# Attention product in 64x64 tiles, FFN products regrouped around x's transposes, and a new order of block 0

## The chip, the cores and the metric

One program runs on one core of a Trainium2 chip. The metric is the device time of one execution in microseconds. The core's engines have instruction queues of their own and wait for each other by semaphores: TensorE (PE, matmuls and transposes; PEld is its loading of weights), VectorE (DVE), ScalarE (ACT), GpSimd (POOL), and SyncE (SP), which here issues the loads and stores.

## What is computed

An attention without softmax, then an FFN with a gate, all in float32:

```python
# q, k, v: (8, 8, 576, 64); x: (4608, 512); d_ff 1536
kv = einsum('bhsd,bhse->bhde', k, v)          # 64x64 for each batch and head
out = einsum('bhsd,bhde->bhse', q, kv)
rms = sqrt(mean(out * out, axis=-1) + 1e-6)
attn = out / rms * g_norm
x = attn.transpose(0, 2, 1, 3).reshape(4608, 512)
g = x @ w_gate
y = (g * sigmoid(g) * (x @ w_val)) @ w_out
```

The three weights come as float64 and are rounded to float32 on the chip.

## The kernel before

The 4608 tokens go through in nine blocks of 512 (`BLK`), four row tiles of 128 each. Since a batch has 576 tokens, block n is cut: in the odd blocks, one row tile of 128 tokens belongs to two batches, 64 tokens each (`parts`).

**Attention of a block** (class `Att`): `load` brings k, v and q; `kv` forms the 64x64 products of k and v, two heads side by side; `turn_q` transposes q; `product(i)` forms q times kv for half a block (i is 0 or 1, two row tiles), squares it on ACT, sums the squares on DVE (`z`) and calls `root`, a chain of eleven short DVE operations that gives 1/sqrt in `y`; then DVE scales the product, out of PSUM, into `xt`. `turn_x(i)` transposes `xt` on PE, and ACT writes it to `x`, which the FFN reads. `sums` forms four sums and differences of quarters of x on DVE.

**FFN of blocks 1 to 8**: seven products of quarter matrices replace eight (Strassen's scheme in Winograd's form). `Up` has a group of seven for each 256 columns of d_ff, `Down` one group for the block, with 12 matmuls of 256 columns in each product. `Down` runs its products in the order 1, 5, 6, 2, 7, 4, 3, and after each one `down` takes one step of the next block's attention from a list (`late`). Differences of weights (tile `t`) are subtracted on GpSimd into six buffers, each as soon as PE has read the older one.

**FFN of block 0** is plain (`plain_up`, `plain_down`), because its weights are still being rounded meanwhile. A piece of weights is 128 columns (or rows of w_out); `Words.round_to` needs two ACT and four DVE operations for it. `t2` then forms one weight sum in place, which the scheme of the later blocks needs.

**What sets the order.** Instructions are emitted in the order of the code, and the framework's scheduler then orders each engine's queue by its own estimates; the engines run their queues strictly in that order. Tiles come from pools: `ld` has seven buffers for every load; PSUM has eight banks, one in pool a, two each in b and c, three in m. All loads are issued on SP in one queue.

Of the kernel before, what the change touches and what calls it, by code (L numbers as in the profile page):

```python
# [18 lines left out]
def kernel(  # L19
# [156 lines left out]
    def round_w(name, j):  # L176
        dst = wviews[name][0]
        words.pop((name, j)).round_to(dst[:, j : j + 1, :] if name == "o" else dst[:, :, P * j : P * (j + 1)])

    class Att:  # L180


        def __init__(self, n):
            self.n = n

            self.cut, half = divmod(n, 2)
            self.split = half * D

        def parts(self, t):
# [7 lines left out]

        def load(self):
            n = self.n
            self.k, self.v, self.q = [], [], []  # L200
            if n < B:
                for j in range(NS):
                    hs = slice(2 * j, 2 * j + 2)
                    for tiles, src in ((self.k, k), (self.v, v)):
                        t = ld_pool.tile([P, 2 * BLK], F32, name="ld")
                        t = t[0:KP, 0 : 2 * KT * D].rearrange("p (h x) -> p h x", h=2)
                        nc.sync.dma_start(
                            out=t, in_=src[n, hs].rearrange("h (p t) d -> p h (t d)", t=KT)
                        )
                        tiles.append(t.rearrange("p h (t d) -> p h t d", t=KT))  # L210
# [36 lines left out]

        def product(self, i):

            ps = [m_psum.tile([P, 2, NS, D], F32, name="m") for _ in range(2)]
            for t in range(2):
                for j in range(NS):
                    for b, _, p0, p1 in self.parts(2 * i + t):
                        for u in range(2):
                            rows = slice(u * D, (u + 1) * D)
                            nc.tensor.matmul(  # L259
                                ps[u][p0:p1, t, j, :], lhsT=self.qt[rows, 2 * i + t, j, p0:p1],  # L260
                                rhs=kvs[b % 3][rows, j, :], start=True, stop=True,
                            )
            z = st_pool.tile([P, 2, 2, NS], F32, name="z")
            for u in range(2):
                sq = sq_pool.tile([P, 2, NS, D], F32, name="sq")
                nc.scalar.activation(out=sq, in_=ps[u], func=ACT.Square)  # L266
                nc.vector.tensor_reduce(out=z[:, u], in_=sq, axis=mybir.AxisListType.X, op=OP.add)  # L267
            y = self.root(z)
            xt = xt_pool.tile([P, 2, NS, 2, D], F32, name="xt")
            for u in range(2):  # L270
                mul(nc.vector, xt[:, :, :, u], ps[u], y[:, u].unsqueeze(3).to_broadcast([P, 2, NS, D]))
            self.xt = xt

        def root(self, z):

            nc.vector.tensor_scalar(out=z, in0=z, scalar1=1.0 / D, scalar2=eps, op0=OP.mult, op1=OP.add)
            y = st_pool.tile([P, 2, 2, NS], F32, name="y")
            nc.vector.tensor_scalar(  # L278
                out=y.bitcast(I32), in0=z.bitcast(I32), scalar1=-0.5, scalar2=float(0x5F3759DF),
                op0=OP.mult, op1=OP.add,  # L280
            )
            a = st_pool.tile([P, 2, 2, NS], F32, name="a")
            for _ in range(3):
                nc.vector.scalar_tensor_tensor(out=a, in0=y, scalar=-0.5, in1=y, op0=OP.mult, op1=OP.mult)  # L284
                nc.vector.tensor_tensor(out=a, in0=a, in1=z, op=OP.mult)  # L285
                nc.vector.scalar_tensor_tensor(out=y, in0=a, scalar=1.5, in1=y, op0=OP.add, op1=OP.mult)  # L286
            return y

# [14 lines left out]
        def sums(self):  # L303
# [52 lines left out]
    class Up(Quad):  # L356
        def __init__(self, ffn, j):
            super().__init__(2)
            self.ffn, self.j = ffn, j
            x, att = ffn.att.x, ffn.att  # L360
            fs = slice(2 * P * j, 2 * P * (j + 1))
            b11, b21, t2, b22 = wg[:, 0:2, fs], wg[:, 2:4, fs], wv[:, 0:2, fs], wv[:, 2:4, fs]
            a11, a12, s2, a22 = x[:, 0:2, 0:HB], x[:, 2:4, 0:HB], x[:, 0:2, HB:BLK], x[:, 2:4, HB:BLK]
# [91 lines left out]
    class Ffn:  # L455
# [28 lines left out]
        def down(self, fill):  # L484
            down = self.down_
            for p in (1, 5, 6, 2, 7, 4, 3):
# [4 lines left out]
                down.multiply(p)  # L491
                if fill:
                    fill.pop(0)()

        def plain_up(self, f):
            ps = []
            for pool, w in ((b_psum, wg), (c_psum, wv)):
                ps.append(pool.tile([P, BLK], F32, name=pool.name[0]))  # L500
                for i in range(NS):
                    nc.tensor.matmul(
                        ps[-1], lhsT=w[:, i, P * f : P * (f + 1)], rhs=self.att.x[:, i, :],
                        start=(i == 0), stop=(i == NS - 1),
                    )
# [35 lines left out]
    blocks = [Att(n) for n in range(NB)]  # L541
    blocks[0].load()
    weights(4)
    for steps in blocks[0].steps():
        for step in steps:
            step()

    for n in range(NB):
        ffn = Ffn(n, blocks[n])
        kv, turn, late = blocks[n + 1].steps() if n + 1 < NB else ([], [], [])  # L550
        if n == 0:
            for f in range(NF):
                weights(2 * (f + 2))
                ffn.plain_up(f)
            weights(len(pieces))
            blocks[1].load()
            for step in kv + turn:
                step()
            for j in range(NP):
                fs = slice(2 * P * j, 2 * P * (j + 1))  # L560
# [45 lines left out]
```

## Time and profile before

| | |
|---|---|
| time, median of 3 runs | 1191.09 us (1190.01 to 1192.87) |
| the profiled execution | 1190.74 us; its span 1189.0 us |
| mean granted clock of TensorE | 0.976 |
| PE busy | 1122.0 us, 94% of the span |
| DVE busy | 404.4 us, 34% |
| ACT busy | 274.5 us, 23% |
| GpSimd busy | 401.7 us, 34% |
| HBM read | 47.19 MB |

In the views quoted below, a timeline row has its start and its duration in us, engine, line, operation, output and inputs, then what ended the engine's idle time before it, in brackets. Equal instructions that follow each other are one row (x24). A float32 matmul leaves two records. A row of windows has the stretch, PE's busy time in it, the granted clock of TensorE, the DMA engines' busy share and GB/s.

### The profile page before, as it was taken

Reading aid. Unit: us, or ns where it says so; the run is one execution under the profiler, and the core shown is the slowest. Engines: PE = TensorE matmul, PEld = TensorE weight load, DVE = VectorE, ACT = ScalarE, POOL = GpSimd, SP = SyncE. Lnnn points to the kernel's source line nnn. Section 1 sums busy time; section 2 is a strip of 40 time slices with the busy share of each in tenths; the row PEclk is TensorE's granted clock in tenths of the full one; section 3 lists DMA queues with packets and bytes.
Section 4 is the critical chain, followed back from the end, with each engine's and each line's share of the span. In section 5 each row is a group of like instructions: output and inputs, shape, how many; then the busy total and the mean of one; then the engine's idle time right before and its main releaser. Section 6 shows DMA issues by size and latency. Waiting matters only on the chain.

```text
span 1189.0 us, 14539 instructions
## 1 busy us (share of the span) xinstructions
PE 1122.0 (94%) x6016; PEld 919.8 (77%) x6016; DVE 404.4 (34%) x770; ACT 274.5 (23%) x468; POOL 401.7 (34%) x320
## 2 busy tenths in 40 slices
PE   3699999998999899998999899989998999999998
PEld 3344456887888788887888788878887888788887
DVE  3466962223321431234112512233214312431221
ACT  3244521221122212221222112211221122112210
POOL 0000221542245324442445145422443245423550
PEclk8699999999999999999999999999999999999999
DMA  9344650210003000400031002100030000000000
GB/s 269 94 141 142 181 128 18 56 41 21 36 19 77 20 19 18 96 21 1 36 86 31 1 36 56 41 20 36 13 69 1 19 18 1 1 1 36 1 1 35
DMA packets 70241, 57.55 MB, mean 48 GB/s; under 512 B 39456, under 2 KB 64032, under 8 KB 70176
## 3 DMA queue, kind: packets, MB, share of 16 engines
q1 hardware_dynamic: 70112, 56.63, 17.6%
q8 instruction: 47, 0.77, 0.3%
q14 instruction: 18, 0.15, 0.0%
q0 software_dynamic: 64, 0.00, 0.0%
HBM read 47.19 MB, written 9.44 MB: 48 GB/s over the span
## 4 chain that ended last, share of the span: by engine, by line
PE 79%; DVE 7%; issue 1%; ACT 1%; DMA 0%; DVEq 0%
PE b L339 43%; PE c L339 18%; PE a L339 8%; PE b L515 3%; PE m L259 3%; DVE y L286 2%; PE m L297 2%; PE m L228 2%; DVE z L267 1%; PE m L242 1%; DVE xt L112 1%; DVE y L278 1%; ACT sq L266 1%; DVE a L284 1%; DVE a L285 1%
## 5 line engine op out<-in xcount | busy, mean ns | idle before, releaser
L111 POOL TENSOR_TENSOR t<-wv 128x512 f32<-128x512 f32 x48 | 66.3, 1382 | 395.9 <-PE b L339 170.7
L111 POOL TENSOR_TENSOR t<-wg,wv 128x512 f32<-128x512 f32 x96 | 123.0, 1285 | 178.1 <-PE c L339 90.6
L111 POOL TENSOR_TENSOR t<-wo 128x512 f32<-128x512 f32 x72 | 91.2, 1267 | 127.5 <-PE c L339 76.3
L110 DVE TENSOR_TENSOR s<-h 128x256 f32<-128x256 f32 x48 | 20.4, 425 | 307.8 <-POOL h L112 307.8
L339 PE MATMUL b<-wo,h 128*128 128x256 f32 x384 | 94.6, 406 | 0.0
L339 PE MATMUL b<-x,wg 128*128 128x256 f32 x384 | 93.1, 382 | 0.0
L339 PE MATMUL b<-x,t 128*128 128x256 f32 x384 | 91.3, 381 | 0.8
L339 PE MATMUL b<-x,wv 128*128 128x256 f32 x384 | 90.7, 379 | 0.0
L339 PE MATMUL c<-xs,t 128*128 128x256 f32 x384 | 90.7, 379 | 0.0
L339 PE MATMUL c<-xs,wv 128*128 128x256 f32 x384 | 90.7, 379 | 0.0
L339 PE MATMUL b<-xs,t 128*128 128x256 f32 x384 | 90.7, 379 | 0.0
L339 PE MATMUL a<-x,wg 128*128 128x256 f32 x384 | 90.7, 379 | 0.0
L339 PEld LDWEIGHTS b<-wo,h 128*128 128x128 f32 x384 | 78.5, 208 | 12.0 <-POOL h L112 0.3
L110 DVE TENSOR_TENSOR u<-c,u 128x512 f32<-128x512 f32 x96 | 65.9, 687 | 63.2 <-ACT u L382 63.2
L339 PE MATMUL b<-t,h 128*128 128x256 f32 x384 | 86.3, 381 | 0.8 <-ACT u L444 0.8
L339 PEld LDWEIGHTS b<-x,t 128*128 128x128 f32 x384 | 72.3, 190 | 12.0 <-issue 2.5
L339 PEld LDWEIGHTS b<-t,h 128*128 128x128 f32 x384 | 71.8, 190 | 12.7 <-issue 3.6
L339 PEld LDWEIGHTS c<-xs,t 128*128 128x128 f32 x384 | 73.0, 190 | 9.9
L339 PEld LDWEIGHTS b<-x,wv 128*128 128x128 f32 x384 | 73.0, 190 | 9.9
L339 PEld LDWEIGHTS a<-x,wg 128*128 128x128 f32 x384 | 73.0, 190 | 9.9
L339 PEld LDWEIGHTS b<-xs,t 128*128 128x128 f32 x384 | 73.0, 190 | 9.9
L339 PEld LDWEIGHTS c<-xs,wv 128*128 128x128 f32 x384 | 73.0, 190 | 9.9
(74 smaller groups left out, 1450.4 us busy)
## 6 DMA issues: line engine op xcount, KB each, us to landing
ld<-in_k_dram SPq DMA_DIRECT2D x32, 288.0 KB, 4.4
ld<-in_v_dram SPq DMA_DIRECT2D x32, 288.0 KB, 3.4
out_dram<-o SPq DMA_DIRECT2D x18, 512.0 KB, 2.8
ld<-in_q_dram SPq DMA_DIRECT2D x32, 256.0 KB, 4.9
ld<-in_moe_w_gate_dram SPq DMA_DIRECT2D x12, 512.0 KB, 6.2
ld<-in_moe_w_val_dram SPq DMA_DIRECT2D x12, 512.0 KB, 4.8
ld<-in_moe_w_out_dram SPq DMA_DIRECT2D x12, 512.0 KB, 3.6
ld<-in_q_dram SPq DMA_DIRECT2D x8, 128.0 KB, 4.2
```

The source lines that it names most:

```text
L110: add = lambda e, o, a, b: e.tensor_tensor(out=o, in0=a, in1=b, op=OP.add)
L111: sub = lambda e, o, a, b: e.tensor_tensor(out=o, in0=a, in1=b, op=OP.subtract)
L112: mul = lambda e, o, a, b: e.tensor_tensor(out=o, in0=a, in1=b, op=OP.mult)
L228: nc.tensor.matmul(self.kv_ps[u * D : (u + 1) * D, j, :], lhsT=self.k[j][:, u, c, :], rhs=self.v[j][:, u, c, :], start=(c == 0), stop=(c = ...
L242: nc.tensor.transpose(ps[:, j], self.q[t][:, j], ident)
L259: nc.tensor.matmul(ps[u][p0:p1, t, j, :], lhsT=self.qt[rows, 2 * i + t, j, p0:p1], rhs=kvs[b % 3][rows, j, :], start=True, stop=True,)
L266: nc.scalar.activation(out=sq, in_=ps[u], func=ACT.Square)
L267: nc.vector.tensor_reduce(out=z[:, u], in_=sq, axis=mybir.AxisListType.X, op=OP.add)
L286: nc.vector.scalar_tensor_tensor(out=y, in0=a, scalar=1.5, in1=y, op0=OP.add, op1=OP.mult)
L297: nc.tensor.transpose(ps[:, e, t], xt[:, t, j + e], ident)
L339: nc.tensor.matmul(self.ps[name][:, e], lhsT=lhsT, rhs=rhs, start=first and (e, i) == (0, 0), stop=i == self.steps - 1, skip_group_check=True,
L515: nc.tensor.matmul(ps, lhsT=self.h[:, f, P * t : P * (t + 1)], rhs=wo[:, f, :], start=(f == 0), stop=(f == NF - 1),)
```

## The change

1. **Product**: every piece of the attention product is cut into output tiles of 64 rows, so that a matmul has 64x64 weights. 16 matmuls of a row tile stand where there were 8.
2. **The list of steps in `Down`**: `half(0)` (product, root, scaling), nothing, `turn_x(0)`, `half(1)`, nothing, and then `turn_x(1)` with `sums`. By the code, two products of the FFN stand between a half and its transposes; before, it was one.
3. **Block 0's attention**: q is loaded ahead of k and v (in every block). In block 0, k and v go to the room of `h` and need no `ld` buffer. `all` runs both halves of the attention at once: one root over both, the second product in banks of pools b and c. One piece of weights is rounded ahead of it, where there were four; the others are to follow the last scaling (`issue_after`).
4. **Weights in tiles**: `wg` and `wv` are six tiles of 256 columns each, no longer one.
5. **Down part of block 0**: `t2` and the first `plain_down` stand ahead of block 1's `kv` and `turn_q`.

PE's queue in the down part of block 1 (`b`, `c`, `a`: PSUM of the FFN's products, in the order 1, 5, 6, 2, 7, 4, 3; `m`: PSUM of the attention; a row counts matmuls). Before:

```order
L339 MATMUL b<-wo,h 128x256 x12
L259 MATMUL m<-kv_112,qt 128x64 x8
L259 MATMUL m<-kv_113,qt 128x64 x8
L339 MATMUL c<-t,s_1189 128x256 x12
L297 MATMUL m<-ident,xt 128x128 x8
L339 MATMUL b<-wo,h 128x256 x12
L259 MATMUL m<-kv_113,qt 128x64 x16
L339 MATMUL a<-wo,h 128x256 x12
L297 MATMUL m<-ident,xt 128x128 x8
L339 MATMUL b<-t,h 128x256 x12
L339 MATMUL b<-x,wg 128x256 x2
L339 MATMUL b<-t,h 128x256 x12
```

The same place now:

```order
L378 MATMUL b<-wo,h 128x256 x12
L271 MATMUL m<-kv_112,qt 64x64 x16
L271 MATMUL m<-kv_113,qt 64x64 x16
L378 MATMUL c<-t,s_1234 128x256 x12
L378 MATMUL b<-wo,h 128x256 x12
L315 MATMUL m<-ident,xt 128x128 x8
L378 MATMUL a<-wo,h 128x256 x12
L271 MATMUL m<-kv_113,qt 64x64 x32
L378 MATMUL b<-t,h 128x256 x12
L378 MATMUL b<-x,wg_114 128x256
L315 MATMUL m<-ident,xt 128x128 x3
L378 MATMUL b<-t,h 128x256 x12
```

The first half's transposes moved behind product 6; of the second half's, three stand behind product 7 and one matmul of the next block, ahead of product 4, and the other five (not shown) behind product 4. It is so in all of blocks 1 to 7.

DVE's queue at the second half of the same block. Before, at that half's end (`y`: the root's last step; `xt`: scaling; `o`, `h`: work behind product 2; `xs`: sums of x):

```order
L286 SCALAR_TENSOR_TENSOR y<-a,y 128x16
L112 TENSOR_TENSOR xt<-m,y 128x8x64 x2
L110 TENSOR_TENSOR o_1543<-a,s 128x2x256
L111 TENSOR_TENSOR h<-h 128x6x256
L110 TENSOR_TENSOR xs<-x 128x512
```

And now, from the first half's scaling to the second half's start (`z`: sums of squares):

```order
L111 TENSOR_TENSOR xt<-m,y 128x8x64 x2
L109 TENSOR_TENSOR o_1588<-a,s 128x2x256
L110 TENSOR_TENSOR h<-h 128x6x256
L281 TENSOR_REDUCE z<-sq 128x8 x2
L287 TENSOR_SCALAR z<-z 128x16
L290 TENSOR_SCALAR y<-z 128x16
```

Product 2's addition into `o` and subtraction on `h` stood behind the second half's scaling; now they stand ahead of its reductions.

DVE's queue in block 0's attention (`a`, `y`: root; `u`, `g`: steps of rounding). Before, in the middle of the first half's root:

```order
L284 SCALAR_TENSOR_TENSOR a<-y 128x16
L150 TENSOR_SCALAR g<-ld 128x512
L285 TENSOR_TENSOR a<-a,z 128x16
L151 SCALAR_TENSOR_TENSOR u_391<-u_391,g 128x512
L286 SCALAR_TENSOR_TENSOR y<-a,y 128x16
L145 TENSOR_SCALAR u_402<-u_402 128x512
L284 SCALAR_TENSOR_TENSOR a<-y 128x16
L150 TENSOR_SCALAR g<-ld 128x512
```

Now, from the last steps of the one root on:

```order
L297 SCALAR_TENSOR_TENSOR a<-y 128x32
L298 TENSOR_TENSOR a<-a,z 128x32
L299 SCALAR_TENSOR_TENSOR y<-a,y 128x32
L111 TENSOR_TENSOR xt<-m,y 128x8x64 x2
L111 TENSOR_TENSOR xt<-b,y 128x8x64
L111 TENSOR_TENSOR xt<-c,y 128x8x64
L144 TENSOR_SCALAR u_366<-u_366 128x512
L149 TENSOR_SCALAR g<-ld 128x512
```

No rounding stands among the root's steps any more; it follows the four scalings, but for the first piece's four operations, which stand ahead of the reductions.

The diff, cut:

```diff
-    wg = consts.tile([P, NS, FF], F32, name="wg")
-    wv = consts.tile([P, NS, FF], F32, name="wv")
+    wg, wv = ([consts.tile([P, NS, 2 * P], F32, name=f"{x}{j}") for j in range(NP)] for x in ("wg", "wv"))
...
+        def load(self, room=None):
+            self.load_q()
...
+                for i, (tiles, src) in enumerate(((self.k, k), (self.v, v))):
+                    if room:
+                        t = room.rearrange("p f t -> p (f t)")[:, (2 * j + i) * 2 * KT * D :]
+                    else:
                         t = ld_pool.tile([P, 2 * BLK], F32, name="ld")
...
-        def product(self, i):
-            ps = [m_psum.tile([P, 2, NS, D], F32, name="m") for _ in range(2)]
+        def product(self, i, pools=None):
+            pools = pools or (m_psum, m_psum)
+            self.ps[i] = [pool.tile([P, 2, NS, D], F32, name=pool.name[0]) for pool in pools]
...
                     for b, _, p0, p1 in self.parts(2 * i + t):
-                        for u in range(2):
-                            rows = slice(u * D, (u + 1) * D)
-                            nc.tensor.matmul(
-                                ps[u][p0:p1, t, j, :], lhsT=self.qt[rows, 2 * i + t, j, p0:p1],
-                                rhs=kvs[b % 3][rows, j, :], start=True, stop=True,
-                            )
+                        for p in range(p0, p1, D):
+                            for u in range(2):
+                                rows = slice(u * D, (u + 1) * D)
+                                nc.tensor.matmul(
+                                    self.ps[i][u][p : p + D, t, j, :],
+                                    lhsT=self.qt[rows, 2 * i + t, j, p : p + D], rhs=kvs[b % 3][rows, j, :],
+                                    start=True, stop=True,
+                                )
...
+        def half(self, i):
+            self.product(i)
+            self.root(i)
+            self.scale(i)
+
+        def all(self):
+            for i in range(2):
+                self.turn_q(i)
+            self.kv(range(NS))
+            self.product(0)
+            self.product(1, (b_psum, c_psum))
+            self.root(0, 2)
+            for i in range(2):
+                self.scale(i)
+                self.turn_x(i)
+            return self.scaled
...
-            late = [
-                lambda: self.product(0), lambda: self.turn_x(0), lambda: self.product(1), lambda: self.turn_x(1),
-            ]
-            return kv, turn, late + ([self.sums] if self.n else [])
+            def last():
+                self.turn_x(1)
+                if self.n:
+                    self.sums()
+            return kv, turn, [lambda: self.half(0), None, lambda: self.turn_x(0), lambda: self.half(1), None, last]
...
-    blocks[0].load()
-    weights(4)
-    for steps in blocks[0].steps():
-        for step in steps:
-            step()
+    room = h_pool.tile([P, NF, BLK], F32, name="h")
+    blocks[0].load(room)
+    weights(1)
+    scaled = blocks[0].all()
...
-                weights(2 * (f + 2))
+                with tc.issue_after(scaled.ins):
+                    weights(2 * (f + 2))
                 ffn.plain_up(f)
             weights(len(pieces))
             blocks[1].load()
+            for j in range(NP):
+                t2(wv[j][:, 0:2], wv[j][:, 2:4], wg[j][:, 0:2])
+            ffn.plain_down(0)
             for step in kv + turn:
                 step()
-            for j in range(NP):
-                fs = slice(2 * P * j, 2 * P * (j + 1))
-                t2(wv[:, 0:2, fs], wv[:, 2:4, fs], wg[:, 0:2, fs])
-            for t in range(T):
+            for t in range(1, T):
                 ffn.plain_down(t)
-                for step in late[2 * t : 2 * t + 2]:
-                    step()
+                for step in late[2 * t - 2 : 2 * t]:
+                    if step:
+                        step()
```

More of the change, by code (lines that the diff above doesn't have):

```diff
@@ L187, in __init__ @@
             self.split = half * D
+            self.ps, self.z = {}, None
         def parts(self, t):
@@ L196, in parts, with load_q @@
             return [(n, first, 0, P)]
[L198 to L204, printed above, removed]
-                        t = ld_pool.tile([P, 2 * BLK], F32, name="ld")
-                        t = t[0:KP, 0 : 2 * KT * D].rearrange("p (h x) -> p h x", h=2)
-                        nc.sync.dma_start(
-                            out=t, in_=src[n, hs].rearrange("h (p t) d -> p h (t d)", t=KT)
-                        )
-                        tiles.append(t.rearrange("p h (t d) -> p h t d", t=KT))
+        def load(self, room=None):
+            self.load_q()
+            self.k, self.v = [], []
+            if self.n == B:
+                return
+            for j in range(NS):
+                hs = slice(2 * j, 2 * j + 2)
+                for i, (tiles, src) in enumerate(((self.k, k), (self.v, v))):
+                    if room:
+                        t = room.rearrange("p f t -> p (f t)")[:, (2 * j + i) * 2 * KT * D :]
+                    else:
+                        t = ld_pool.tile([P, 2 * BLK], F32, name="ld")
+                    t = t[0:KP, 0 : 2 * KT * D].rearrange("p (h x) -> p h x", h=2)
+                    nc.sync.dma_start(out=t, in_=src[self.n, hs].rearrange("h (p t) d -> p h (t d)", t=KT))
+                    tiles.append(t.rearrange("p h (t d) -> p h t d", t=KT))
+        def load_q(self):
+            self.q = []
             for i in range(2):
@@ L281, in root @@
             )
-            a = st_pool.tile([P, 2, 2, NS], F32, name="a")
+            flat = lambda t: t.rearrange("p i u t j -> p (i u t j)")
+            y, a, z = flat(y), flat(a), flat(z)
             for _ in range(3):
@@ L286, in root, with scale @@
                 nc.vector.scalar_tensor_tensor(out=y, in0=a, scalar=1.5, in1=y, op0=OP.add, op1=OP.mult)
-            return y
+        def scale(self, i):
+            self.xt = xt_pool.tile([P, 2, NS, 2, D], F32, name="xt")
+            for u in range(2):
+                y = self.y[:, i, u].unsqueeze(3).to_broadcast([P, 2, NS, D])
+                self.scaled = mul(nc.vector, self.xt[:, :, :, u], self.ps[i][u], y)
         def turn_x(self, i):
@@ L491, in down @@
                 down.multiply(p)
-                if fill:
-                    fill.pop(0)()
+                step = fill.pop(0) if fill else None
+                if step:
+                    step()
         def plain_up(self, f):
```

32 lines of the change are left out of this document (16 added, 16 removed).

## The prediction

> **What bounds the kernel now.** I read the page first, its busy times and the chain that ended last:
> ```profile
> PE 1122.0 (94%) x6016; PEld 919.8 (77%) x6016; DVE 404.4 (34%) x770; ACT 274.5 (23%) x468; POOL 401.7 (34%) x320
> ...
> PE 79%; DVE 7%; issue 1%; ACT 1%; DMA 0%; DVEq 0%
> ```
> PE bounds the kernel, so time comes off only where it idles, runs slowly or has less to do. The list of its waits (us in total, times, longest) says where it idles:
> ```profile
> PE m L297 <- DVE xt L112: 47.5, 15, 14.6
> PE m L228 <- DMA ld<-in_v_dram: 12.7, 6, 5.4
> ```
> Nearly all idle time stands before x's transposes (L297), which wait for VectorE's scaled `xt`. The rest waits for v. The timeline of the lead-in and of block 0:
> ```profile
> 13.36 1.55 PE L228 MATMUL m<-ld 96*64 96x64 f32 x24 [0.92 <-DMA ld<-in_v_dram]
> ...
> 35.20 1.94 PE L297 MATMUL m<-ident,xt 128*128 128x128 f32 x8 [14.62 <-DVE xt L112]
> ...
> 37.07 3.68 PE L259 MATMUL m<-kv,qt 64*128 64x64 f32 x32
> ...
> 46.53 1.94 PE L297 MATMUL m<-ident,xt 128*128 128x128 f32 x8 [5.78 <-DVE xt L112]
> ...
> 48.39 5.66 PE L502 MATMUL b<-x,wg 128*128 128x512 f32 x8
> ...
> 53.89 3.60 PE L502 MATMUL c<-x,wv 128*128 128x512 f32 x8
> ...
> 134.12 1.88 PE L515 MATMUL b<-wo,h 128*128 128x512 f32 x4
> 138.38 0.92 PE L228 MATMUL m<-ld 96*64 96x64 f32 x24 [2.38 <-DMA ld<-in_v_dram]
> ...
> 150.10 0.92 PE L228 MATMUL m<-ld 96*64 96x64 f32 x24 [1.64 <-DMA ld<-in_v_dram]
> ...
> 192.85 1.89 PE L339 MATMUL b<-x,wg 128*128 128x256 f32 x8
> ```
> The FFN starts only at 48.4, its down part at 134.1, block 1's at 192.9. In each of blocks 1 to 7 the down part then looks like this (block 1):
> ```profile
> 278.17 5.45 PE L339 MATMUL c<-t,s 128*128 128x256 f32 x24
> ...
> 280.31 1.26 POOL L111 TENSOR_TENSOR t<-wo 128x512 f32<-128x512 f32 x1 [6.95 <-PE c L339]
> 280.42 1.18 DVE L278 TENSOR_SCALAR y<-z 128x16 int32<-128x16 int32 x1
> ...
> 282.04 1.26 POOL L111 TENSOR_TENSOR t<-wo 128x512 f32<-128x512 f32 x1 [0.46 <-PE c L339]
> 282.06 1.27 DVE L286 SCALAR_TENSOR_TENSOR y<-a,y 128x16 f32<-128x16 f32 x1
> ...
> 285.79 1.29 DVE L112 TENSOR_TENSOR xt<-m,y 128x512 f32<-128x512 f32 x2
> ...
> 287.23 1.32 PE L297 MATMUL m<-ident,xt 128*128 128x128 f32 x8 [3.61 <-DVE xt L112]
> ...
> 288.34 6.82 PE L339 MATMUL b<-wo,h 128*128 128x256 f32 x24
> 295.09 2.00 PE L259 MATMUL m<-kv,qt 64*128 64x64 f32 x32
> ...
> 297.75 1.28 DVE L267 TENSOR_REDUCE z<-sq 128x8 f32<-128x512 f32 x2 [10.67 <-ACT sq L266]
> ...
> 301.43 1.29 DVE L112 TENSOR_TENSOR xt<-m,y 128x512 f32<-128x512 f32 x2
> 302.64 0.68 DVE L110 TENSOR_TENSOR o<-a,s 128x512 f32<-128x512 f32 x1
> ...
> 302.87 1.06 PE L297 MATMUL m<-ident,xt 128*128 128x128 f32 x8 [0.40 <-DVE xt L112]
> 303.24 1.75 DVE L111 TENSOR_TENSOR h<-h 128x1536 f32<-128x1536 f32 x1
> ...
> 303.77 5.35 PE L339 MATMUL b<-t,h 128*128 128x256 f32 x24
> ...
> 307.54 1.26 POOL L111 TENSOR_TENSOR t<-wv 128x512 f32<-128x512 f32 x1 [22.51 <-PE b L339]
> 308.76 2.49 POOL L111 TENSOR_TENSOR t<-wg,wv 128x512 f32<-128x512 f32 x2
> ...
> 309.83 0.69 DVE L110 TENSOR_TENSOR o<-c,u 128x512 f32<-128x512 f32 x1 [2.19 <-ACT u L444]
> ```
> Three things are to be seen. First, the first half's chain takes 8.9 us from the product's end (about 278.2) to 287.1, and one FFN product of 5.4 covers it badly; the second half's takes 5.7 (297.0 to 302.7) and is nearly covered. Second, the difference is GpSimd: each time it subtracts `t`, the 0.17 us step of VectorE's root that comes next ends with it, 1.2 us late (280.42, 282.06, and once more). The addition at 309.83, which reads PSUM, is not held up by GpSimd's two operations from 308.76 on. Third, the idle time costs twice, since the clock falls behind it; the windows by the microsecond:
> ```profile
> 288.00:289.00 1.00, 1.00 (x5) 0.50 0.06 16
> ```
> So product 6 takes 6.82 instead of 5.3, and from 278.17 to 295.09 pass 16.9 us, where two products (5.25 each) and 0.95 of transposes would be 11.5: 5.4 lost, of which 3.6 is wait and 1.8 clock.
>
> **The sum** is made against the profiled execution: span 1189.0, its own time 1190.74, which is 0.35 under the median of the three runs.
>
> *Product in 64x64 tiles.* Block 3's first product already has one of its two row tiles cut so, 32 of its 48 records:
> ```profile
> 402.90 1.73 PE L259 MATMUL m<-kv,qt 64*128 64x64 f32 x48
> 404.56 5.45 PE L339 MATMUL c<-t,s 128*128 128x256 f32 x24
> ```
> 48 records pass in 1.66 us from start to start, the 32 of an uncut product in 1.93 (295.09 to 297.02). A row tile in four quarters thus costs 1.66 - 0.97 = 0.69 against 0.97: 0.27 less, though it has twice the matmuls. Seven blocks have 28 row tiles here, three cut already: 25 x 0.27 = 7 us off PE's own path. The Trainium skill, TensorEngine Tiling (Array Packing), Available Configurations, gives two tiles to 64x128 and four to 64x64; twice the matmuls over twice the tiles would gain nothing, this term would be 0 and the sum 1167. Block 3's rows disagree, and they decide.
>
> *First half, blocks 1 to 7.* Products 5 and 6 now both stand between: 10.5 us over a chain of 8.9. GpSimd's three subtractions fall into product 5 as before, so the chain stays as long. The wait goes, and with it the slow clock: 7 x 5.4 = 38 off. Cover is left over by 1.5 us.
>
> *Second half, blocks 1 to 7.* The diff puts products 7 and 4 between; the built program does not. On PE's queue only product 7 and one matmul of the next block (0.43) stand ahead of three of the eight transposes, and product 4 is queued behind these, so PE waits if xt is late. Against product 7's start as zero: on VectorE product 2's addition and its 1.75 us subtraction on h now stand ahead of the reductions. Product 2 ends at -1.4, so the two last from -1.2 to 1.15 (0.60 and 1.75, rows 302.64 and 303.24), and the reductions start there instead of at 0.75. From a reduction's start to xt's end are 4.97 us (297.75 to 302.72), 2.4 of them the root's eleven steps (299.03 to 301.43): 6.1 if nothing interferes. But GpSimd's subtractions for the next block start 3.77 behind product 7's start (303.77 to 307.54) and run back to back; so far VectorE was through by then, now its root is at its seventh step of eleven. I take what the first half shows: each GpSimd operation holds one step to its end. Three of 1.25 end at about 5.0, 6.3 and 7.6, with one step between them; two steps (0.4) and xt (1.3) follow: xt ends at 9.3. PE is there at 5.7. The wait is 3.7 instead of 0.40, and the slow clock behind it costs 1.8, as behind 3.6. That is 7 x (3.3 + 1.8) = 36 on. Bounds: 0.5 with no collision, 1.7 with one and no clock loss, 4.1 if no step gets between. What ends last is one place later than before, at nearly the same price.
>
> *Lead-in.* q, k and v are 3.4 MB. Two windows show the rates while k, v and then q arrive:
> ```profile
> 10.00:11.00 1.00, 0.34 (x7) 1.00 1.11 270
> ...
> 13.00:14.00 1.00, 0.64 (x12) 1.00 1.33 215
> ```
> Now 1.05 MB of q at 215 GB/s come first (4.9 us), then 2.36 MB at 270 (8.7), from 2 us on: 15.6, say 16.5, since weights mix in. Before, v came at 13.4 with q still open; bounds 14 and 18. The last group of kv (1.55) and its copy end at 18.5; both products, 1.4 to 2.8 each by clock, at about 23. The squares stand on ScalarE behind the rounding's steps of the first two weight pieces, whose 1 MB lands 3 us behind v; so four squares, four reductions, one root and four scalings, about 10 us of short steps, end at 31 instead of 46.4. But four roundings had been done by then and now one has: the matmuls with wv need pieces v0 and v1, and three roundings lie on the path:
> ```profile
> 142.24 0.68 DVE L155 CUSTOM_DVE_ANT_0 wo<-u,u 128x1024 uint16<-128x1024 uint16 x1
> ...
> 150.42 0.68 DVE L155 CUSTOM_DVE_ANT_0 wo<-u,u 128x1024 uint16<-128x1024 uint16 x1
> ```
> Four more pieces end in 8.2 us, one other operation of 0.6 among them: 1.9 each. Piece v1 is there at about 37.4, when five of 96 matmuls are done. From 53.89 to 134.12 are 23 groups of four: 3.49 each. 91 matmuls take 79.4, less the few waits and with a slow first stretch as at 48.39 (5.5 instead of 3.5): the up part ends at 117, not 134. VectorE's 32 pieces (61), 12 products with h and 12 operations on wv (0.6 each, 14) make 75 beside PE's 79 and hide; without that cover see the second rival. 17 off; bounds 10 and 21.
>
> *Down part of block 0.* The first product over wo runs before kv and covers the loads: 4.0 of waits and some slow clock go, the two products save 0.8. A load of v that has no buffer until the first kv is through costs 0.5 again; the sums of x now stand behind two 1.76 us operations on wo on VectorE, 0.8. 5 off, bounds 2 and 7.
>
> q ahead of k and v on SP's queue in later blocks holds two of seven buffers longer; v's third load then waits for the first kv, and 12 us of matmuls lie between: nothing.
>
> Sum: -17 -5 -7 -38 +36 = -31; 1190.7 - 31 = 1160.
>
> **Rivals.** (1) The second half's chain is covered: GpSimd and VectorE alternate more finely than I think, or GpSimd starts later. For it: the chain alone misses by only 0.5. Against: each collision of the first half above cost the whole operation. 36 less: 1124; with one collision 1135.
> (2) The lead-in's gain is lost to VectorE: if a piece costs 2.5, a third more than above, 32 pieces and 14 us more end at 132, behind PE's 117; the down part can hide eight of that. 8 to 17 back: 1168 to 1177. Against: the 1.9 above.
> (3) Slower than before: a product wholly in 64x64 tiles does not keep the cut row tile's pace of 22 ns a record but the uncut one's of 62. Then a row tile costs 2.0, 1.3 more than counted, and 32 of them (25, block 0's four, three in its down part) cost 41: 1201. It turns the sign from about 50 ns a record on. For it: no product here is wholly so. Against: rows 402.90 and 404.56.
> (4) The change does not do what it says: PE still waits before the first half's transposes. It needs a chain over 10.5 us, two more GpSimd operations in it; the first half would cost 5 again: 1195.
>
> **How the numbers follow.** My forecast 66% (1148 to 1172 by its bounds), the covered second half 20%, VectorE-bound lead-in 7%, slow tiles 3%, first half still open 4%. Taking in most of rival (1) down to its price and leaving out (3) and (4), the range is 1124 to 1172. About 0.2% (2.4 us) is what a measurement can tell from no change: faster 0.93, same 0.02, slower 0.05.
>
> **What would show it.** Waits of PE: `xt` about 30 us in all, seven or eight times near 3.7, all before the transposes behind product 7, with GpSimd's `t<-wv` beside the held root steps and the clock at 0.50 behind; no wait behind product 6. The first wv matmuls near 33 and the first wo matmul near 117; the first block-1 matmul near 170. Each uncut product about 1.4 from start to start. I am wrong if VectorE's root slips between GpSimd's operations, or if h's products in block 0 run late.

## The result, and the profile after

The changed kernel takes 1154.19 us (median of four runs, 1151.48 to 1157.04), beside 1191.62 us for the kernel before on the same chip: a ratio of 0.9687, 95% interval 0.9652 to 0.9721. The prediction said 1160 (1124 to 1172). The profiled execution, the fastest of the four, took 1151.48 us with a span of 1149.7, where the one before had 1190.74 and 1189.0; the mean granted clock went from 0.976 to 0.983.

From the page of the changed kernel, busy time and the chain that ended last, and from its list of PE's waits (us in total, times, longest):

```profile
PE 1103.0 (96%) x6528; PEld 906.0 (79%) x6528; DVE 422.2 (37%) x759; ACT 272.2 (24%) x468; POOL 399.2 (35%) x320
...
PE 91%; DVE 6%; DMA 1%; issue 1%; SPq 1%; ACT 0%; DVEq 0%
...
PE m L315 <- DVE xt L111: 30.3, 8, 5.8
PE m L237 <- DMA h<-in_v_dram: 3.4, 4, 1.2
```

The wait for `xt` has fallen from 47.5 us in 15 pieces to 30.3 in 8: one of 5.8 in block 0, and one of 3.5 in each of blocks 1 to 7. PE's row of the timeline in block 0:

```profile
30.08 3.68 PE L315 MATMUL m<-ident,xt 128*128 128x128 f32 x16 [5.81 <-DVE xt L111]
33.68 2.08 PE L541 MATMUL b<-x,wg 128*128 128x512 f32 x2
...
117.25 2.31 PE L554 MATMUL b<-wo,h 128*128 128x512 f32 x5
...
169.13 1.89 PE L378 MATMUL b<-x,wg 128*128 128x256 f32 x8
```

The FFN starts at 33.7 (before 48.4), its down part at 117.3 (134.1), block 1's FFN at 169.1 (192.9). The down part of block 1, by PE, VectorE and GpSimd:

```profile
252.91 1.16 PE L271 MATMUL m<-kv,qt 64*64 64x64 f32 x64
...
261.63 1.29 DVE L111 TENSOR_TENSOR xt<-m,y 128x512 f32<-128x512 f32 x2
...
264.47 1.04 PE L315 MATMUL m<-ident,xt 128*128 128x128 f32 x8
265.35 5.34 PE L378 MATMUL a<-wo,h 128*128 128x256 f32 x24
270.62 1.16 PE L271 MATMUL m<-kv,qt 64*64 64x64 f32 x64
...
271.34 1.75 DVE L110 TENSOR_TENSOR h<-h 128x1536 f32<-128x1536 f32 x1
271.71 5.45 PE L378 MATMUL b<-t,h 128*128 128x256 f32 x24
...
273.00 1.27 DVE L281 TENSOR_REDUCE z<-sq 128x8 f32<-128x512 f32 x2
...
275.58 1.30 POOL L110 TENSOR_TENSOR t<-wv 128x512 f32<-128x512 f32 x1 [14.71 <-PE b L378]
275.78 1.13 DVE L299 SCALAR_TENSOR_TENSOR y<-a,y 128x16 f32<-128x16 f32 x1
...
276.85 2.48 POOL L110 TENSOR_TENSOR t<-wg,wv 128x512 f32<-128x512 f32 x2
276.95 1.19 DVE L297 SCALAR_TENSOR_TENSOR a<-y 128x16 f32<-128x16 f32 x1
277.00 0.59 PE L378 MATMUL b<-x,wg 128*128 128x256 f32 x2
278.17 1.19 DVE L298 TENSOR_TENSOR a<-a,z 128x16 f32<-128x16 f32 x1
...
279.67 1.29 DVE L111 TENSOR_TENSOR xt<-m,y 128x512 f32<-128x512 f32 x2
281.11 0.52 PE L315 MATMUL m<-ident,xt 128*128 128x128 f32 x3 [3.52 <-DVE xt L111]
281.46 7.03 PE L378 MATMUL b<-t,h 128*128 128x256 f32 x24
288.33 0.71 PE L315 MATMUL m<-ident,xt 128*128 128x128 f32 x5
...
295.36 1.89 PE L378 MATMUL c<-xs,t 128*128 128x256 f32 x8
```

An uncut product now passes in 1.10 us from start to start. The first half's `xt` ends at 262.9, the transposes come at 264.47 and have no wait. In the second half each of GpSimd's three subtractions holds one of VectorE's 0.17 us steps to its own end; `xt` is late, PE stands for 3.52 us and then runs product 4 in 6.87 us from start to start, not in 5.2.

That slow stretch differs from block to block. The two groups of transposes around product 4 in block 3 and in block 4, and windows in blocks 1, 3 and 4 (stretch, PE's busy time, granted clock, DMA):

```profile
528.91 0.52 PE L315 MATMUL m<-ident,xt 128*128 128x128 f32 x3 [3.50 <-DVE xt L111]
...
534.45 0.71 PE L315 MATMUL m<-ident,xt 128*128 128x128 f32 x5
...
651.31 0.87 PE L315 MATMUL m<-ident,xt 128*128 128x128 f32 x3 [3.50 <-DVE xt L111]
...
659.68 0.71 PE L315 MATMUL m<-ident,xt 128*128 128x128 f32 x5
...
282.00:283.00 1.00, 1.00 (x3) 0.50 0.00 0
530.00:531.00 1.00, 1.00 (x7) 1.00 0.00 0
656.00:657.00 1.00, 1.00 (x4) 0.50 0.00 0
```

After the same wait of 3.50, block 3 loses nothing (5.54 us between the two groups of transposes), block 4 loses 2.83 (8.37). Over the seven blocks it is 1.68, 1.33, 0, 2.83, 1.67, 2.76 and 1.67: 11.9 us, 1.7 in the mean.

### The profile page after: what moved, and what is told of

It reads as the page before. It is cut to its first block, busy times and chain, and to the rows that moved or that the text cites. A ratio compares the mean times of both kernels' runs of the same rounds, so it can differ in the third digit from the quotient of the medians.

```text
span 1149.7 us, 15520 instructions
## 1 busy us (share of the span) xinstructions
PE 1103.0 (96%) x6528; PEld 906.0 (79%) x6528; DVE 422.2 (37%) x759; ACT 272.2 (24%) x468; POOL 399.2 (35%) x320
## 4 chain that ended last, share of the span: by engine, by line
PE 91%; DVE 6%; DMA 1%; issue 1%; SPq 1%; ACT 0%; DVEq 0%
PE b L378 41%; PE c L378 22%; PE a L378 11%; PE b L541 4%; PE c L541 4%; PE b L554 4%; PE m L237 2%; PE m L315 2%; PE m L251 1%; PE m L271 1%; DVE h L110 1%; DVE a L297 1%; DVE a L298 1%; DVE y L299 1%; DVE z L281 1%
## 5 line engine op out<-in xcount | busy, mean ns | idle before, releaser
L110 POOL TENSOR_TENSOR t<-wv 128x512 f32<-128x512 f32 x48 | 63.4, 1320 | 364.1 <-PE b L378 152.0
L378 PE MATMUL b<-t,h 128*128 128x256 f32 x384 | 96.7, 414 | 0.8 <-ACT u L482 0.8
L378 PEld LDWEIGHTS b<-t,h 128*128 128x128 f32 x384 | 79.7, 211 | 13.8 <-issue 1.2
L378 PE MATMUL b<-wo,h 128*128 128x256 f32 x384 | 85.9, 379 | 0.0
L393 ACT COPY u<-b 128x512 f32<-128x512 f32 x56 | 32.8, 586 | 214.2 <-PE b L378 214.2
```

The lines of the kernel that those rows point to most:

```text
L110: sub = lambda e, o, a, b: e.tensor_tensor(out=o, in0=a, in1=b, op=OP.subtract)
L378: nc.tensor.matmul(self.ps[name][:, e], lhsT=lhsT, rhs=rhs, start=first and (e, i) == (0, 0), stop=i == self.steps - 1, skip_group_check=True,
L393: nc.scalar.copy(out=self.u2, in_=self.ps["b"])
```

## The experiments

Ratios are to the kernel before on the same chip, with 95% intervals. The first three take the forecast's chief claim apart: why does PE still wait in the second half, and what is the wait worth?

### e1_turn_behind_4: the second half's transposes where the code has them

```diff
                 if step:
-                    step()
+                    with tc.issue_after(self.down_.last.ins):
+                        step()
```

(`last` is the latest matmul of the product.)

> The changed kernel, with the second half's eight transposes of x held behind product 4 on PE's queue in blocks 1 to 7, where the code has them. Theory (the program waits because the scheduler moved three of the eight ahead of product 4): product 4 covers the chain, the seven waits of 3.5 us go (24.5) and with them the slow clock behind them (12.1 in the changed kernel's trace: the five transposes behind product 4 start 5.54 to 8.37 us after the first three, 5.5 without loss). 37 less: about 1117 us, no wait of PE before x's transposes outside of block 0. Rival: the wait moves on, to the next block's product 5, which needs the sums of x, formed behind these transposes: product 3 and product 1 (7 us) stand between, and ACT's two copies and VectorE's sums take 4.5 if nothing holds them; if GpSimd holds each sum up by 1.2, up to 2 us a block come back: about 1131.

Measured: 1115.26 us, ratio 0.9369 (0.9351 to 0.9388). VectorE and PE in block 1:

```profile
278.32 5.42 PE L378 MATMUL b<-t,h 128*128 128x256 f32 x24
278.50 1.19 DVE L298 TENSOR_TENSOR a<-a,z 128x16 f32<-128x16 f32 x1
...
280.00 1.29 DVE L111 TENSOR_TENSOR xt<-m,y 128x512 f32<-128x512 f32 x2
...
283.58 1.04 PE L315 MATMUL m<-ident,xt 128*128 128x128 f32 x8
```

GpSimd still holds three steps and `xt` is as late as before, but product 4 stands ahead of the transposes and covers it with 2.3 us to spare. The wait is gone in all seven blocks, the mean granted clock of the profiled execution is 1.0, and the next block's sums are in time, so the rival falls. What the changed kernel gave away, 36 us by the spans and 39 by the medians, hung on three transposes that the scheduler put ahead of a product. This is the fastest version run.

### e2_t_behind_scaling: GpSimd waits, the queues stay

```diff
-                sub(nc.gpsimd, t[-1], b, t2)
+                s = sub(nc.gpsimd, t[-1], b, t2)
+                if j == 0:   # the first group of a block
...
+                    tc.add_manual_dep(s.ins, att.scaled.ins.name, dep, reason="behind the scaling")
```

(`dep` describes the dependency.)

> The changed kernel, with GpSimd's three subtractions for the next block's first group waiting for the end of the second half's scaling (xt); PE's and VectorE's queues stay as they are. Theory (each GpSimd subtraction holds up one step of VectorE's root): with GpSimd silent, xt ends 6.1 us after product 7's start instead of 9.3, PE is there at 5.7, the wait falls from 3.5 to about 0.5 and the slow clock behind it goes: 7 x 3.0 + 12 = 33 less, about 1121 us. Rival (VectorE's addition and 1.75 us subtraction of product 2, which now stand ahead of the reductions, are the cause): xt ends hardly earlier, the waits stay above 2 us, 1142 to 1154. Either way the three subtractions end about 10 us after product 7's start, and the next block needs the first of them at 19: no new wait.

Measured: 1123.27 us, ratio 0.9436 (0.9414 to 0.9459). Block 1:

```profile
282.14 0.17 DVE L299 SCALAR_TENSOR_TENSOR y<-a,y 128x16 f32<-128x16 f32 x1
282.42 1.29 DVE L111 TENSOR_TENSOR xt<-m,y 128x512 f32<-128x512 f32 x2
283.85 0.52 PE L315 MATMUL m<-ident,xt 128*128 128x128 f32 x3 [0.52 <-DVE xt L111]
283.88 1.27 POOL L110 TENSOR_TENSOR t<-wv 128x512 f32<-128x512 f32 x1 [17.27 <-DVE xt L111]
```

All eleven steps of the root take 0.17 to 0.18 us when GpSimd is silent, the wait is 0.52 in every block, and no slow clock follows. VectorE's own queue was the same, so the rival falls: GpSimd is what makes the chain late. The time is 2 us above the forecast, and its "no new wait" failed in block 1: there GpSimd's subtractions, which the changed kernel had done by 108 us, now start at 164.85 and hold up VectorE's two operations on `wo` (2.61 and 2.71 us, 1.76 in the changed kernel); the sums of x come late, PE waits 2.88 for them, and the next two groups of its matmuls take 2.54 and 2.67 in place of 1.73.

### e11_down2_last: VectorE's own part

```diff
         def after2(self):
+            pass
+        def late2(self):
             add(nc.vector, self.o1[:, :, 0:HD], self.ps["a"], self.s)
...
+                if p == 2 and fill:
+                    with tc.issue_after(blocks[self.n + 1].scaled.ins):
+                        down.late2()
...
```

> The changed kernel with VectorE's two operations of product 2 (the addition into o and the 1.75 us subtraction on h) queued behind the second half's scaling, GpSimd as it is. Theory (the number of GpSimd operations that the root meets sets the wait; the two operations only shift the root against them): the reductions start 0.7 us after product 7's start in place of 1.3, the root is at its tenth step when GpSimd starts at 3.9, so two steps are held up in place of three, as in e6's trace, and the wait is 2.0 in place of 3.5, short enough to keep the clock, as the waits of 2.48 in e6 did in six of seven blocks: 7 x (1.5 + 1.7) = 22 less, about 1132 us. Rival A (these two operations are the whole cause): the wait falls under 0.6, 1121. Rival B (they don't matter): 3.5 as before, 1154; or product 3 waits for the subtraction on h, which it reads, and time comes back there.

Measured: 1137.41 us, ratio 0.955 (0.953 to 0.9571). Two held steps in block 1, and the second half of block 4:

```profile
276.96 1.22 DVE L298 TENSOR_TENSOR a<-a,z 128x16 f32<-128x16 f32 x1
278.22 1.18 DVE L299 SCALAR_TENSOR_TENSOR y<-a,y 128x16 f32<-128x16 f32 x1
...
280.94 0.52 PE L315 MATMUL m<-ident,xt 128*128 128x128 f32 x3 [2.04 <-DVE xt L111]
...
643.77 0.52 PE L315 MATMUL m<-ident,xt 128*128 128x128 f32 x3 [2.05 <-DVE xt L111]
...
651.00 0.71 PE L315 MATMUL m<-ident,xt 128*128 128x128 f32 x5
```

Its reductions start 0.75 us after product 7 and not 1.29, so the root is at its tenth step when GpSimd begins: two steps are held and not three, and the wait is 2.04, as expected. The two operations of product 2 matter only by shifting the root against GpSimd. The 5 us above the forecast are the clock: a wait of 2.05 was still followed by a slow stretch in four of seven blocks (7.23 us between the transposes in block 4, 5.54 without), 4 x 1.69 = 6.8.

### e4_filler and e4b_filler7: the wait filled

```diff
...
+                if p == 7 and fill:
+                    idle = a_psum.tile([P, 2, HB], F32, name="a")
+                    with tc.issue_after(down.last.ins):
+                        for k in range(15):          # e4b: 7
+                            filler = nc.tensor.matmul(
+                                idle[:, k % 2], lhsT=self.h[:, 1, HB + P : BLK], rhs=wo[:, 1, 0:HD],
+                                start=True, stop=True,
+                            )
+                    with tc.issue_after(filler.ins):
+                        turned = fill.pop(0)()       # the eight transposes
```

> The changed kernel with 15 matmuls of 128x256 that nothing reads put into PE's queue behind product 7 in blocks 1 to 7 (3.2 us at 0.216 each), ahead of all eight transposes of the second half and these ahead of product 4. The chain is as late as before, only the wait is filled. Theory (the slow clock follows from PE's idle time, and costs 12.1 us in the changed kernel's trace): the granted clock stays at 1.00 behind the wait, the wait shrinks to about 0.7, and with the chain's end as it was the time falls by those 12: about 1142 us, and the scatter from run to run (1151.5 or 1157) goes. Rival (the clock falls for another reason than idleness): 1152 to 1157 as without them. Second rival: the filler delays the transposes, since 15 take more than 3.2: above 1157.

Measured: 1159.75 us, ratio 0.9744 (0.9724 to 0.9764). The expectation took a record for a matmul, as this row shows (30 records for 15 matmuls, 6.47 us to the next start):

```profile
278.89 6.64 PE L542 MATMUL a<-wo,h 128*128 128x256 f32 x30
```

The filler outlasted the wait, and cost 6.5 where wait and slow clock had cost 5.2. So again, with seven:

> As e4_filler, with 7 filler matmuls in place of 15: e4's trace shows that a matmul of 128x256 passes in 0.43 us, twice what its expectation had (0.216 is one of its two records), so 15 took 6.46 us and outlasted the wait. Theory (idleness of PE slows the clock behind it): 7 x 0.43 = 3.0 us fill most of the wait; the clock stays at 1.00; xt ends 9.2 to 9.4 us after product 7's start as before, PE is there at 8.3. A block's second half then loses 4.0 us in place of 5.2 (3.5 of wait and 1.7 of slow clock): 7 x 1.2 = 9 less, about 1143 to 1145 us. Rival (the slow clock has another cause): the wait that is left is followed by products of 6.4 to 7 us, 1154 to 1158.

Measured: 1143.11 us (1142.69 to 1143.28), ratio 0.9604 (0.959 to 0.9618). Block 1:

```profile
277.71 3.19 PE L542 MATMUL a<-wo,h 128*128 128x256 f32 x14
281.81 1.06 PE L315 MATMUL m<-ident,xt 128*128 128x128 f32 x8 [0.92 <-DVE xt L111]
282.71 5.35 PE L379 MATMUL b<-t,h 128*128 128x256 f32 x24
```

Work that nothing reads makes the kernel 11 us faster: `xt` is as late as before, but product 4 runs in 5.2 us, and the mean granted clock is 0.999. So the slow clock follows from idleness, and it is a price of its own beside the wait. The edit also keeps all eight transposes ahead of product 4, which has no run of its own; e3 (below) speaks against this as the cause, since eight transposes stand together there behind waits of 3.08 to 3.09 us, and five of seven blocks are slowed. The four runs lie within 0.6 us; those of the changed kernel spread over 5.6. That this spread is the clock too is not shown: its two runs near 1151.5 have a mean granted clock of 0.983, the two near 1157 have 0.984 and 0.980.

### e3_tiles_only, e6_list_only, e5_block0_only: the parts alone

e3 puts the loop `for p in range(p0, p1, D)` of the diff into the kernel before. e6 changes its list of steps only:

```diff
+            if self.n > 1:
+                def last():
+                    self.turn_x(1)
+                    self.sums()
+                late = [late[0], None, late[1], late[2], None, last]
...
```

e5 is the changed kernel with the product uncut and, in blocks 1 to 7, the old list.

> The kernel before, with nothing but the attention product cut into 64x64 tiles. The prediction's term: 25 uncut row tiles in blocks 1 to 7 times 0.27 us = 7, so 1184.5 us. By the changed kernel's trace (64 records in 1.10 us from start to start against 32 in 1.93, 0.42 a row tile): 10.4, so 1181 us. Rival: twice as many matmuls over twice as many tiles gain nothing: 1191. Second rival: the product gets shorter, but PE then waits longer before the transposes, since these wait for VectorE: the wait would grow from 3.6 to 4.4 in the first half and 0.4 to 1.2 in the second, and nothing is gained, 1191.

Measured: 1169.17 us, ratio 0.9833 (0.9802 to 0.9864): 21.6 us, three times what the prediction's term gave and twice the second estimate. The trace gives 3.9 of it to block 0 and 18.0 to blocks 1 to 8: 10.8 are the 14 shorter products, and 5.5 are waits, since in blocks 1 to 7 the scheduler moved one matmul of the next FFN product ahead of the transposes; the rest is not split up. The first half's wait is 3.09 (before 3.61), the second half's none:

```profile
406.37 1.09 PE L298 MATMUL m<-ident,xt 128*128 128x128 f32 x8 [3.09 <-DVE xt L112]
```

> The kernel before with the new list of steps in the down part of blocks 1 to 7 alone (part 2 of the change), products uncut. PE's queue: the first half's transposes behind product 6; of the second half's, seven behind product 7 alone. Theory: the first half's wait and slow clock go (7 x 5.4 = 38 less); the second half's wait becomes 3.9 (xt 9.2 us after product 7's start, PE there at 5.3), with some 1.7 of slow clock behind it: 7 x (3.5 + 1.7) = 36 more. About nothing: 1189, between 1184 and 1196. Rival (the regrouping brought most of the change's gain): 1155 to 1165.

Measured: 1167.62 us, ratio 0.981 (0.9795 to 0.9825). A miss: the expectation was 1189. The second half of block 1:

```profile
295.94 1.28 DVE L267 TENSOR_REDUCE z<-sq 128x8 f32<-128x512 f32 x2 [0.20 <-ACT sq L266]
...
299.08 1.27 POOL L111 TENSOR_TENSOR t<-wv 128x512 f32<-128x512 f32 x1 [15.55 <-PE b L347]
299.14 1.25 DVE L285 TENSOR_TENSOR a<-a,z 128x16 f32<-128x16 f32 x1
300.42 1.19 DVE L286 SCALAR_TENSOR_TENSOR y<-a,y 128x16 f32<-128x16 f32 x1
...
303.14 0.95 PE L297 MATMUL m<-ident,xt 128*128 128x128 f32 x7 [2.48 <-DVE xt L112]
```

The wait is 2.48 in six of the seven blocks (2.04 in block 6, where three transposes stand ahead), not 3.9. I had taken the chain's timing from the changed kernel, where the product is 0.83 us shorter. Here the longer product hides VectorE's 1.75 us subtraction: the reductions start 0.7 us after product 7 (which starts at 295.21), GpSimd meets the tenth step, and two steps are held. The clock stayed up in six of seven blocks. So the list alone brings 22.5 us, and the two edits work against each other: in the second half the shorter product saves 0.83 us of PE, but moves the root so that a third step is held.

> The kernel before with the edits to block 0 alone (parts 3 to 5 of the change): uncut products, and in blocks 1 to 7 the steps of the down part as before. Theory: as in the changed kernel, where block 1's first matmul moved from 192.85 to 169.13 (23.7 us), less what the uncut products of block 0 cost: two of 3.7 at half clock instead of 5.1 us together, and 0.8 each in the down part: about 20 less, 1171 us, with the waits before x's transposes in blocks 1 to 7 as before (3.6 and 0.40 a block). Rival (VectorE's 32 roundings bound block 0, as the prediction's second rival had it, and the gain needs the shorter products): under 10 less, above 1180.

Measured: 1170.9 us, ratio 0.9841 (0.9825 to 0.9857), block 1's first matmul at 173.11: as expected.

Alone, the three parts bring 21.6, 22.5 and 19.2 us, each near 2% with an interval wholly below 1, together 63; the change brought 37. With the transposes behind product 4 (e1) it is 75.

### e7, e12, e8, e10: block 0 taken apart

Each undoes an edit of block 0 in the changed kernel (e12 two; in short form):

```diff
-    weights(1)
+    weights(4)                                      # e7, e12
-                with tc.issue_after(scaled.ins):    # e12: free to go anywhere
-                    weights(2 * (f + 2))
+                weights(2 * (f + 2))
+            if self.n == 0: self.load_q()           # e8: behind k and v
-            self.product(1, (b_psum, c_psum))       # e10: two halves in turn
-            self.root(0, 2)
+            for i in range(2): self.half(i); self.turn_x(i)
```

> The changed kernel with four pieces of weights ahead of block 0's attention instead of one; the rest still behind the last scaling. On VectorE's queue three more pieces stand between the first two reductions and ahead of the others. Theory: the fourth piece lands near 26 and is rounded at 28; then two reductions, root and scaling end at 35 to 36 instead of 31.1, the FFN starts 4 us later, and its first wv matmuls never waited, so nothing comes back: about 1158 us, first wg matmul at 37 to 38 instead of 33.7. Rival (rounding ahead is free, since it fills VectorE's idle time while q, k and v arrive): 1154 us, first wg matmul near 34.

> The changed kernel with four pieces ahead of block 0's attention and the others free to go anywhere, as in the kernel before: on VectorE's queue 13 operations of rounding now stand among the root's eleven steps as well. Theory (the lead-in's gain comes from taking the rounding out of the root): 13 x 0.6 = 8 us more on top of four pieces ahead: first wg matmul at 44 to 46, about 10 to 11 us in all, 1164. Rival (the gain comes from q ahead, from the room of h for k and v, and from one root for both halves): 1154 to 1158, first wg matmul before 38.

> The changed kernel with block 0's q loaded behind k and v again. Theory (the product needs all three, 3.4 MB, whatever comes first): k and v land near 12 us and q near 17; the transposes of q then stand where the last group of kv stood; the first product starts within 2 us of 19.05, at 18 to 21; the total moves by under 2 us: 1152 to 1157. Rival (q ahead is a part of the lead-in's gain): the transposes of q at half clock and their copies (3.7 and 0.7) come on top of the landing: product at 22 to 23, 1158.

> The changed kernel with block 0's attention in two halves, one after the other, each with its own root, and the second product back in the m banks. Theory: the second product has to wait for the first half's scaling to free its banks (about 27.7), its squares, reductions, root and scaling end near 35 in place of 31.1; the first wg matmul at 36 to 37 in place of 33.7: 3 us more, 1157. Rival (both roots fit into the time that VectorE idles while the squares come): 1154, first wg matmul before 34.5.

First matmul with wg, with wo, and of block 1 on PE's timeline (us), and the time:

| | wg | wo | block 1 | time, ratio (interval) |
|---|---|---|---|---|
| before | 48.39 | 134.12 | 192.85 | |
| changed | 33.68 | 117.25 | 169.13 | 1154.19, 0.9687 (0.9652 to 0.9721) |
| e7, four pieces ahead | 37.89 | 121.03 | 173.13 | 1158.73, 0.9737 (0.9722 to 0.9751) |
| e12, and the rest free | 42.66 | 125.60 | 177.54 | 1162.32, 0.9768 (0.9753 to 0.9783) |
| e8, q last | 38.05 | 121.13 | 173.04 | 1155.75, 0.9713 (0.9696 to 0.973) |
| e10, two roots | 38.05 | 122.61 | 174.42 | 1158.6, 0.974 (0.9722 to 0.9757) |

The pieces ahead cost 4.0 us at block 1's first matmul, as expected. Freeing the rest costs 4.4 more, not 8: the wg matmul comes at 42.7, not 44 to 46. With q last, its 16 transposes wait until 14.9 and the first product starts at 22.9: the rival holds, q ahead is worth 3.9 us in the trace, though the medians differ by 1.6, less than the changed kernel's own spread. Two roots cost 5.3, more than the 3 expected. So no single edit made the gain up to block 1: rounding last (8.4), one root (5.3) and q ahead (3.9) are 17.6 of 23.7 us, and the shorter products are 4.0 more by e5, where block 1 begins at 173.11. Undone one by one, they need not add up. The room of h for k and v, the weights in tiles and the order of the down part were not undone singly.

## Why the prediction was right, term by term

Block 1's second half before ended, for this count, at the next block's first matmul with the sums of x:

```profile
321.24 1.89 PE L339 MATMUL c<-xs,t 128*128 128x256 f32 x8
```

| term | predicted | measured in the two traces |
|---|---|---|
| product in 64x64 tiles | -7 | -10.8 |
| first half, blocks 1 to 7 | -38 | -38.5 |
| second half, blocks 1 to 7 | +36 | +33.3 |
| lead-in | -17 | -16.9 |
| down part of block 0 | -5 | -6.9 |
| sum | -31 | -39.8 (the span: -39.3) |

*Product.* The mechanism held, the size was off: I took block 3's cut row tile as 1.66 less half an uncut product, 0.69 us; a row tile in quarters takes 0.55 (1.10 for two), 17 ns a record. 11 uncut products save 0.83 each and three half cut ones 0.56. The third rival (62 ns a record) is refuted by the row at 252.91, 64 records in 1.10 us.

*First half.* From product to product 276.24 to 295.09 were 18.85 us; the same work takes 12.44 now (252.91 to 265.35). Over seven blocks that is 44.0 less, 5.5 of it the product. The cover left over is 1.6 us, predicted 1.5. The fourth rival falls.

*Second half.* From product to sums 295.09 to 321.24 were 26.15 us; now 24.74 (270.62 to 295.36), and product 2, which stands ahead (5.27), makes it 30.01. Over seven blocks 28.1 more, and 33.3 with the product's 5.3 taken out. The wait came as told: three steps held, 3.50 in every block (predicted 3.7), 1.7 of slow clock (1.8). The first rival, a covered second half at 1124, needed what e1 and e2 did by hand. What the prediction did not see is that this loss belongs to tiles and list together: e6 shows 15.3 (the same count in its trace) for the list alone.

*Lead-in and down part.* The up part ended at 117.25 (117 predicted), block 1 began at 169.13 (near 170). VectorE's last rounding ended at 115.7, ahead of PE, so the second rival falls. In one step the number held by some luck: the prediction put three roundings on the path, with PE at five of 96 matmuls when piece v1 is there at 37.4. Piece v1 came at 37.8, but no matmul with `wv` waited: the first starts at 35.55, once v0 is there (33.8). PE had done three matmuls by 37.4, and then needed 0.858 us for each, not 0.873; the two misses, 1.7 and 1.3 us, nearly cancel.

Of the 8.5 us between 1160 and the profiled 1151.48, 3.8 are the product, 2.7 the second half and 1.9 the down part.

## What to carry to other kernels

Read from the built queue, not from the code, what stands between a chain's start and its use; three hoisted transposes cost half of a gain of 75 us, and pinning them behind the product gave it back. Where a short chain on VectorE meets a train of GpSimd operations, count how many of its steps start after GpSimd does: a shift of half a microsecond decides between two held steps and three, so an edit that shortens the work ahead can lengthen the wait. And price PE's idle time with the slow clock behind it; if a wait can't be removed, even work that is thrown away can pay, as long as it ends before the wait does (here seven matmuls won 11 us and fifteen lost 6).

## What the runs showed of the hardware

**The slow clock comes in stretches of about 3.4 us, and the wait ahead of one need not be that long.** The first and the last window of the slow stretch in block 4 of e11, behind a wait of 2.05 us:

```profile
644.00:645.00 1.00, 1.00 (x6) 0.58 0.00 0
...
647.00:648.00 1.00, 1.00 (x5) 0.71 0.00 0
```

The two windows between are at 0.50. At half clock a mean of 0.58 is 0.84 us and a mean of 0.71 is 0.58 us; with the two whole windows these are 3.42 us, which cost 1.7. In the changed kernel, windows of half a microsecond put the starts of the slow stretches of blocks 1, 2 and 4 at 281.6, 404.5 and 650.3; they last 3.4, 3.4 and 6.8 us, and the second and the third start 36 and 108 times 3.41 us behind the first.

After waits of 3.50 us (changed kernel) six of seven blocks were slowed, by 1.3 to 2.8 us; after 3.08 (e3, first half) five of seven; after 2.48 (e6) one of six; after 2.05 (e11) four of seven, by 1.69; after 0.92 (e4b) and 0.52 (e2) none. The Trainium skill, TensorE: Matmul & The Clock Gate, What's actually happening, has a free-running window of 3.4 us and lets the clock fall after at least one idle window. The starts of the stretches, their lengths and the change from block to block agree with a free-running window; that it takes a whole idle one does not agree with the 2.05 us waits.

**GpSimd holds VectorE by whole operations, one short step to each.** With three GpSimd subtractions back to back in the changed kernel, each held exactly one 0.17 us step of the root, in all seven blocks; the wait was the same 3.50 to 3.52. The Trainium skill, SBUF — State Buffer, Who interferes with whom, calls the port pair that VectorE and GpSimd share an exclusive lock. The traces agree: a held step lasts 1.13 to 1.28 us and ends with the GpSimd operation, and in e2 the same eleven steps take 0.17 to 0.18 us each.
